# Linear attention, routed experts and a gated layer in one kernel: small loads moved to another queue, norms regrouped, rank products and w1 splits reordered

## The chip, the cores and the metric

One core of a Trainium2 chip runs the whole program. Its engines are PE (TensorE: matrix products and transposes into PSUM), ACT (ScalarE), DVE (VectorE), POOL (GpSimd) and SP (SyncE, which here only issues transfers); transfers run on 16 DMA engines. The metric is the time of one execution on the device in microseconds (us); less is better.

## The reference

```python
# attention without softmax, 4 batches x 8 heads x 576 tokens x 64
kv  = einsum('bhsd,bhse->bhde', k, v)
out = einsum('bhsd,bhde->bhse', q, kv)
x   = out / sqrt(mean(out*out, -1) + 1e-6) * g_norm       # -> 2304 tokens x 512

# 8 experts, the best two of each token
noisy = x @ w_gate + log1p(exp(x @ w_noise)) * noise
top2, top2_w = best two of noisy, softmax over them
x = sum over the two: top2_w * (relu(x @ w1[e]) @ w2[e])  # w1 512x1024, w2 1024x512

# gated layer
h = x @ w_in                                              # 512 x 2048
return (h * sigmoid(h)) @ w_out                           # 2048 x 512
```

## The kernel before

The 2304 tokens are handled as two halves, b = 0 and 1, of 1152 tokens (two attention batches each): 128 partitions times J = 9 tokens. JJ = 5 units `jj` hold tokens 2jj and 2jj+1, the last one only token 8.

**Loads.** `load_qkv(b)` (line 123) issues 8 pairs of k and v and then 8 loads of q on SP's queue, 288 KB each. In program order come then, on the same queue, `gcol` (g_norm, lines 135 and 136), the two halves of `wg_raw` (w_gate and w_noise, lines 138 and 139), `noise_sb` (line 650) and `load_qkv(1)`. Two DVE operations make `gw`, the gate weights times g_norm (line 144).

**Attention.** `kv_of` makes the products of k and v of one batch, `turn_kv` transposes them, `gates_of` multiplies them with `gw`, so that the gate's logits come out of the same product as the attention output; it therefore needs `gw`. `q_of` transposes two tokens' q by PE into `qT`, which ACT copies out of PSUM. `out_of(b, jj, hf)` makes half a unit of the output: 8 heads in two halves of four, so a full half takes 16 short products, ACT's copy `o` (line 435), ACT's square `sq` (line 439) and DVE's sum `ss` (line 440). `out_all(b, between)` runs the ten halves n = 0 to 9, puts a `q_of` behind each of n = 0, 2 and 4, and calls whatever `between` has for n.

**Norms, routing, lists.** `norm(b, group)` computes 1/sqrt of the mean squares for a group of units by a bit trick and three Newton steps of three DVE operations (lines 480 to 482), then the group's logits (`pl`, line 486, and the reduction `lg`, line 491). The groups are units 0 to 2 (six tokens, after n = 5) and units 3, 4 (three tokens, after the last half). `store_x` scales the output to `xh` (line 450) and SP stores it to `x_dram` (line 456). `route(b)` is a generator run piece by piece by `run(b)`: (1) noisy logits and the best two experts, ending in `rowtot`; (2) the rank product `rk` on PE and, on DVE, the ranks, ending in `ohb` (line 604); (3) the list product `ids_ps` on PE, which gives the token lists, `ids_early` for batch 0 and `ids` for both (line 626); (4) the weights of the two experts. `behind(ins)` keeps instructions of the same engine behind `ins`; `marked[b]` is the last one marked by `norm` or `route`, `listed[b]` the write of the list.

**The turn to the experts.** While batch 1 is ranked, PE works for expert 0 on the tokens of batch 0: `early_x` gathers two tiles by `ids_early` (POOL, line 228), transposes them (`xt`) and ACT scales them to `xe` (line 310); `early_h(f)`, f = 0 to 7, are the first layer's products in full float32, evicted by ACT (line 734); `early_y(a)`, a = 0 and 1, the second layer's, eight steps of two passes each. `early_y(1)` has the transposes of the remaining tiles 2, 3 and 4 of expert 0 between its steps 4, 5 and 6; these tiles are gathered from all of `x_dram` by `ids`. Then `mm1` of expert 0 follows, which needs w1 of expert 0 split in a high part (ACT, line 202) and a low part (DVE, line 203).

**Order.** PE runs in the order of the program. ACT and DVE run in that order only where `act` and `dve` are used; where the text has `nc.scalar` or `nc.vector`, a planner that simulates the time line orders them. Behind the turn come eight experts and the gated layer, which the change does not touch.

Of the kernel before, what the change touches and what calls it, by code (L numbers as in the profile page):

```python
# [8 lines left out]
F32 = mybir.dt.float32  # L9
# [5 lines left out]
ALU = mybir.AluOpType  # L15
# [4 lines left out]
P = 128  # L20
PT = 128
# [26 lines left out]
def attention_moe_mlp(  # L48
# [15 lines left out]
    nc = tc.nc  # L64
    pe, act, dve = (InOrder(tc, engine) for engine in (nc.tensor, nc.scalar, nc.vector))

    NB, H, SB, D = q.shape
    B, S = NB // 2, 2 * SB
    N, DM = out.shape
    E, _, F = w1.shape  # L70
    DFF = w_in.shape[1]
    J = S // PT
    JJ = (J + 1) // 2
# [22 lines left out]
    def psB(name):  # L96
        return psum.tile([P, 512], F32, tag="B", name=name)
# [35 lines left out]
    make_identity(nc, ident)  # L133
    gcol = const.tile([P, 1], F32, name="gcol")
    for r in range(2):
        nc.sync.dma_start(gcol[r * D : (r + 1) * D, :], g_norm.rearrange("(d o) -> d o", o=1))
    wg_raw = const.tile([P, HP, 2, E], F32, name="wg_raw")
    nc.sync.dma_start(wg_raw[:, :, 0, :], w_gate.rearrange("(c p) e -> p c e", p=P))
    nc.sync.dma_start(wg_raw[:, :, 1, :], w_noise.rearrange("(c p) e -> p c e", p=P))
    gw = const.tile([P, HP, 4 * E], F32, name="gw")  # L140
    nc.vector.memset(gw, 0.0)
    for r in range(2):
# [75 lines left out]
    def behind(ins):  # L218
        return tc.issue_after(ins.ins) if ins else ExitStack()
# [43 lines left out]
    def store_y(e, a, py, eng):  # L263
        y = mp.tile([P, DM], F32, tag="y", name=f"y{e}_{a}", bufs=2)
        eng.activation(y, py, AF.Copy)
        if a < HA // P:
            eng.dma_start(y_first[e * HA + a * P : e * HA + (a + 1) * P, :], y)
        eng.dma_start(y_dram[e * CAP + a * P : e * CAP + (a + 1) * P, :], y)
# [38 lines left out]
    def early_x():  # L307
        for a in range(HA // P):
            xv = turn_x(gather_x(0, a, x_dram[0 : EB * S, :], ids_early[:, a : a + 1]), psB(f"xt0_{a}"))
            nc.scalar.activation(xe[:, :, a * P : (a + 1) * P], xv, AF.Identity, scale=gcol)  # L310

    raw1, raw2, h0 = [], [], []
    listed, marked, stored = {}, {}, []

    def early_y(a, between):

        py = psB(f"py0_{a}")
        for f in range(KF):
            if f in between:
                between[f]()  # L320
            pe.matmul(
                py, h0[f][:, a * P : (a + 1) * P], raw2[f // 2][:, f % 2 * DM : (f % 2 + 1) * DM],
                start=(f == 0), stop=(f == KF - 1),
            )
        store_y(0, a, py, nc.scalar)

    with ExitStack() as ph1:
        att = ph1.enter_context(tc.tile_pool(name="att", bufs=1))
        wk = ph1.enter_context(tc.tile_pool(name="wk", bufs=2))
# [48 lines left out]
        def q_of(b, jj):  # L378

            j0 = min(2 * jj, J - 2)  # L380
            qps = psA(f"qps{b}_{jj}")
            for r in range(2):
                for hp in range(HP):
                    pe.transpose(
                        qps[:, r, hp * P : (hp + 1) * P],
                        qkv["q", 2 * b + r, hp][:, j0 : j0 + 2, :].rearrange("p j d -> p (j d)"),
                        ident,
                    )
            qT[b, jj] = att.tile([P, 2, HP * P], F32, tag="qT", name=f"qT{b}_{jj}", bufs=3)
            nc.scalar.activation(qT[b, jj], qps, AF.Copy)  # L390
# [21 lines left out]
        def tokens_of(jj):  # L412

            return 2 * jj, min(2, J - 2 * jj)

        def out_of(b, jj, hf):

            j0, n = tokens_of(jj)
            if hf == 0:
                raw[b, jj] = att.tile([P, H, n * 80], F32, tag=f"o{n}", name=f"o{b}_{jj}", bufs=4 if n > 1 else 1)  # L420
            if b not in ss:
                ss[b] = wk.tile([P, J, H], F32, name="ss")
            po = psA(f"po{b}_{jj}_{hf}")
            w = n * 80
            for m in range(4):
                h = hf * 4 + m
                for r in range(2):
                    pe.matmul(
                        po[r * D : (r + 1) * D, m // 2, (m % 2) * w : (m % 2 + 1) * w],
                        qT[b, jj][:, r, h * D : (h + 1) * D],  # L430
                        kvbds[2 * b + r][:, h, 160 - w :],
                        start=True, stop=True,
                    )
            rows = raw[b, jj][:, hf * 4 : (hf + 1) * 4, :]
            nc.scalar.activation(
                rows.rearrange("p (a c) d -> p a (c d)", a=2), po[:, :, : 2 * w], AF.Copy
            )
            sq = wk.tile([P, 4, n, D], F32, tag="sq", name="sq", bufs=2)
            nc.scalar.activation(sq, rows.rearrange("p h (r c) -> p h r c", r=n)[:, :, :, :D], AF.Square)
            nc.vector.tensor_reduce(  # L440
                ss[b][:, j0 : j0 + n, hf * 4 : (hf + 1) * 4].rearrange("p r h -> p h r"),
                sq, axis=AX.X, op=ALU.add,
            )
# [17 lines left out]
        def norm(b, jjs):  # L461

            if b not in rinv:
                rinv[b] = wk.tile([PT, J, H], F32, name="rinv")
                logits[b] = wk.tile([PT, J, 2 * E], F32, name="lg", bufs=1)
            units = [tokens_of(jj) for jj in jjs]
            js = slice(units[0][0], sum(units[-1]))
            nj = js.stop - js.start

            ms = wk.tile([PT, 6 * H], F32, name="ms", bufs=1)[:, : nj * H]  # L470
            nc.vector.tensor_scalar(
                ms, ss[b][:, js].rearrange("p j h -> p (j h)"), 1.0 / D, EPS, op0=ALU.mult, op1=ALU.add
            )
            rf = rinv[b][:, js].rearrange("p j h -> p (j h)")
            ri = rf.bitcast(I32)
            nc.vector.tensor_single_scalar(ri, ms.bitcast(I32), 1, op=ALU.arith_shift_right)
            nc.vector.tensor_scalar(ri, ri, -1.0, float(0x5F3759DF), op0=ALU.mult, op1=ALU.add)
            t0 = wk.tile([PT, 6 * H], F32, name="t0", bufs=1)[:, : nj * H]
            for _ in range(3):
                nc.vector.tensor_mul(t0, rf, rf)  # L480
                nc.vector.scalar_tensor_tensor(t0, t0, -0.5, ms, op0=ALU.mult, op1=ALU.mult)
                nc.vector.scalar_tensor_tensor(rf, t0, 1.5, rf, op0=ALU.add, op1=ALU.mult)

            pl = wk.tile([P, 6, H, 2 * E], F32, name="pl", bufs=1)[:, :nj]
            for jj, (j0, n) in zip(jjs, units):
                nc.vector.tensor_mul(
                    pl[:, j0 - js.start : j0 - js.start + n],
                    raw[b, jj].rearrange("p h (r c) -> p r h c", r=n)[:, :, :, D:],
                    rinv[b][:, j0 : j0 + n, :, None].to_broadcast([P, n, H, 2 * E]),
                )  # L490
            marked[b] = nc.vector.tensor_reduce(logits[b][:, js], pl.rearrange("p j h c -> p j c h"), axis=AX.X, op=ALU.add)

        def route(b):
# [153 lines left out]
            yield  # L647

        noise_sb = const.tile([PT, B, J, E], F32, name="noise_sb")
        nc.sync.dma_start(  # L650
            noise_sb.rearrange("p b j e -> p b (j e)"),
            noise.rearrange("(b p j) e -> p b (j e)", b=B, j=J),
        )
# [3 lines left out]
        def run(b):  # L657
            if b not in step:
                step[b] = route(b)
            next(step[b])  # L660

        GROUPS = (range(3), range(3, JJ))

        def out_all(b, between):

            for n in range(2 * JJ):
                out_of(b, *divmod(n, 2))
                if n % 2 == 0 and n // 2 + 2 < JJ:
                    q_of(b, n // 2 + 2)
                if n in between:  # L670
                    between[n]()
                if n == 5:
                    norm(b, GROUPS[0])

        def store_behind(b, jjs):
            with behind(marked[b]):
                store_x(b, jjs)
# [9 lines left out]
        gates_of(1)  # L687
        q_of(0, 1)
        out_all(0, {})
        norm(0, GROUPS[1])  # L690
        store_behind(0, (0,))
        run(0)
# [13 lines left out]

        def rank_first():
            run(0)
            store_behind(0, GROUPS[1])

        out_all(1, {2: rank_first, 5: lambda: run(0)})
        early_x()
        norm(1, GROUPS[1])
        store_behind(1, (0,))
        run(1)
# [19 lines left out]

        for f in range(KF):
            early_h(f)
            if f == 6:
                run(1)
                store_behind(1, GROUPS[1])  # L740
        early_y(0, {3: lambda: run(1)})
        with behind(marked[B - 1]):
            w1_sb[0] += [split(raw1[c], f"w1_0_{c}", nc.scalar, nc.vector) for c in range(KD)]
        with behind(listed[B - 1]):
            run(B - 1)
# [555 lines left out]
```

## Time and profile before

| | before |
|---|---|
| median of 3 runs | 1001.96 us (1001.76 to 1007.46) |
| the profiled execution, whole | 995.8 us |
| its span, first to last instruction | 994.0 us |
| PE busy | 955.5 us (96%) |
| DVE busy | 500.3 us (50%) |
| ACT busy | 327.9 us (33%) |
| POOL busy | 252.1 us (25%) |
| mean granted clock of PE | 0.992 |

A busy share is a mean over the whole span; a stage can look different. In a time line, a row has the start and the length in us, the engine (SPq is SP's queue), the line of the source (L44 is the helper through which all ordered instructions are recorded), the operation, what it writes and reads, and how many rows of the same kind were merged; in brackets how long the engine had been idle and what ended that. Float32 products run as two passes and count twice. PEclk is the granted clock as a share of 2.4 GHz: 1.00 is 2.4 GHz, 0.50 is 1.2 GHz.

### The profile page before, as it was taken

Reading aid. Unit: us, or ns where it says so; the run is one execution under the profiler, and the core shown is the slowest. Engines: PE = TensorE matmul, PEld = TensorE weight load, DVE = VectorE, ACT = ScalarE, POOL = GpSimd, SP = SyncE. Lnnn points to the kernel's source line nnn. Section 1 sums busy time; section 2 is a strip of 40 time slices with the busy share of each in tenths; the row PEclk is TensorE's granted clock in tenths of the full one; section 3 lists DMA queues with packets and bytes.
Section 4 is the critical chain, followed back from the end, with each engine's and each line's share of the span. In section 5 each row is a group of like instructions: output and inputs, shape, how many; then the busy total and the mean of one; then the engine's idle time right before and its main releaser. Section 6 shows DMA issues by size and latency. Waiting matters only on the chain. (4 is left out here: it accounts for less than half of the span.)

```text
span 994.0 us, 14472 instructions
## 1 busy us (share of the span) xinstructions
PE 955.5 (96%) x5586; PEld 818.1 (82%) x5586; DVE 500.3 (50%) x949; ACT 327.9 (33%) x499; POOL 252.1 (25%) x271
## 2 busy tenths in 40 slices
PE   5988899999999999999999999999999999999997
PEld 4867599889798897989889789888888888888886
DVE  2488648675766766666674355332333332232221
ACT  1773254333333333333333244222321231223212
POOL 3000255535444454544520131001100010100000
PEclk9998999999999999999999999999999999999999
DMA  9862637484755747466471573101110020101001
GB/s 318 282 233 76 215 121 232 141 273 126 235 180 161 242 128 253 150 202 199 131 246 49 165 226 94 43 1 43 40 46 21 22 85 1 43 1 43 0 1 44
DMA packets 65096, 127.01 MB, mean 128 GB/s; under 512 B 11264, under 2 KB 19456, under 8 KB 65024
## 3 DMA queue, kind: packets, MB, share of 16 engines
q1 hardware_dynamic: 50880, 91.44, 28.6%
q0 software_dynamic: 6080, 19.93, 6.5%
q10 hardware_dynamic: 8064, 14.68, 4.0%
q8 instruction: 45, 0.74, 0.3%
q14 instruction: 27, 0.22, 0.1%
HBM read 92.94 MB, written 33.08 MB: 127 GB/s over the span
## 5 line engine op out<-in xcount | busy, mean ns | idle before, releaser
L44 PE MATMUL ph<-xT,hw 128*128 128x256 f32 (+1 forms) x960 | 212.5, 312 | 0.1
L44 PE MATMUL py<-hw,h 128*128 128x512 f32 x608 | 199.8, 400 | 7.6 <-DVE h L44 5.4
L44 PE MATMUL pout<-hwout,g 128*128 128x512 f32 x576 | 191.8, 395 | 0.0
L44 PE MATMUL pg<-x2T,hwin 128*128 128x512 f32 (+1 forms) x640 | 184.2, 373 | 0.0
L44 PEld LDWEIGHTS ph<-xT,hw 128*128 128x128 f32 x960 | 162.6, 189 | 1.8 <-DVE xT L44 0.6
L44 DVE TENSOR_TENSOR sg<-pg,sg 128x512 f32<-128x512 f32 x72 | 49.8, 692 | 211.0 <-ACT sg L44 211.0
L44 PE MATMUL ph<-xT,lw 128*128 128x256 f32 (+1 forms) x480 | 149.8, 312 | 0.0
L44 PEld LDWEIGHTS py<-hw,h 128*128 128x128 f32 x608 | 114.4, 188 | 35.5 <-DVE h L44 8.1
L44 PEld LDWEIGHTS pg<-x2T,hwin 128*128 128x128 f32 x640 | 116.6, 189 | 23.4 <-DVE x2T L44 0.2
L44 PEld LDWEIGHTS pout<-hwout,g 128*128 128x128 f32 x576 | 108.2, 188 | 24.3
L44 PE MATMUL py<-lw,h 128*128 128x512 f32 x304 | 119.9, 394 | 0.0
L44 PE MATMUL pg<-x2T,lwin 128*128 128x512 f32 (+1 forms) x320 | 119.0, 372 | 0.0
L44 ACT ACTIVATE sg<-pg 128x512 f32<-128x512 f32 x72 | 43.1, 598 | 217.1 <-PE pg L44 217.1
L44 PE MATMUL pout<-lwout,g 128*128 128x512 f32 x288 | 112.9, 392 | 0.0
L1010 POOL DMA_INDIRECT yg<-y_dram,rt x32 | 31.8, 993 | 261.1 <-PE x2ps L44 219.0
L44 DVE SCALAR_TENSOR_TENSOR h<-ph,h 128x640 fp32r<-128x640 f32 (+1 forms) x64 | 50.5, 789 | 82.5 <-ACT h L44 78.2
L44 ACT ACTIVATE h<-ph 128x640 fp32r<-128x640 f32 (+1 forms) x64 | 43.5, 679 | 144.3 <-PE ph L44 135.7
L44 PEld LDWEIGHTS ph<-xT,lw 128*128 128x128 f32 x480 | 90.6, 189 | 0.0
L1093 POOL TENSOR_TENSOR w<-w,bits 128x256 f32<-128x256 f32 x64 | 47.3, 740 | 143.4 <-DVE w L44 143.2
L44 DVE TENSOR_TENSOR g<-sg,g 128x512 fp32r<-128x512 f32 x72 | 49.8, 692 | 44.7 <-ACT g L44 44.7
L203 POOL TENSOR_TENSOR lw<-rw,hw 128x1024 fp32r<-128x1024 f32 x28 | 67.4, 2409 | 17.0 <-ACT hw L44 17.0
L44 PEld LDWEIGHTS pg<-x2T,lwin 128*128 128x128 f32 x320 | 60.4, 189 | 11.5
(173 smaller groups left out, 1082.4 us busy)
## 6 DMA issues: line engine op xcount, KB each, us to landing
rw<-in_moe_w_dram SPq DMA_DIRECT2D x56, 512.0 KB, 4.0
y_dram<-y ACTq DMA_DIRECT2D x40, 256.0 KB, 4.1
f<-in_moe_w_in_dram SPq DMA_DIRECT2D x32, 256.0 KB, 3.6
f<-in_moe_w_out_dram SPq DMA_DIRECT2D x32, 256.0 KB, 3.0
k<-in_k_dram SPq DMA_DIRECT2D x16, 288.0 KB, 6.0
v<-in_v_dram SPq DMA_DIRECT2D x16, 288.0 KB, 6.3
q<-in_q_dram SPq DMA_DIRECT2D x16, 288.0 KB, 6.0
out_dram<-ob SPq DMA_DIRECT2D x18, 256.0 KB, 3.5
```

The source lines that it names most:

```text
L44: return lambda *args, **kwargs: self.tc.keep_in_program_order(op(*args, **kwargs))
L203: low.tensor_sub(lo, raw, hi.bitcast(F32))
L1010: nc.gpsimd.indirect_dma_start(out=y, out_offset=None, in_=src, in_offset=bass.IndirectOffsetOnAxis(ap=self.rt[:, t, kk : kk + 1].bitcast( ...
L1093: nc.gpsimd.tensor_add(w, w, bits.bitcast(F32))
```

## The change

Five small loads (`gcol` twice, `wg_raw` twice, `noise_sb`) are issued from ScalarE's queue instead of SP's. A norm's group 0 now has units 0 and 1 (four tokens, computed after half n = 3), group 1 units 2 to 4 (five tokens). The three Newton steps (nine operations) become a third-order step and one Newton step (seven operations); the buffers shrink from six to five tokens. In batch 1's `out_all` the rank product of batch 0 moves from behind half 2 to behind half 0, and the list product from behind half 5 to behind half 3. The rank product of batch 1 moves from behind `early_h(6)` to behind `early_h(7)`, its list product from before step 3 to before step 6 of `early_y(0)`. The stores behind them keep their units 3 and 4. The splits of w1 of expert 0 stand behind `listed` instead of `marked`, so on DVE behind the write of the lists instead of behind `ohb`.

```diff
--- before.py
+++ after.py
@@ -133,10 +133,10 @@
     make_identity(nc, ident)
     gcol = const.tile([P, 1], F32, name="gcol")
     for r in range(2):
-        nc.sync.dma_start(gcol[r * D : (r + 1) * D, :], g_norm.rearrange("(d o) -> d o", o=1))
+        nc.scalar.dma_start(gcol[r * D : (r + 1) * D, :], g_norm.rearrange("(d o) -> d o", o=1))
     wg_raw = const.tile([P, HP, 2, E], F32, name="wg_raw")
-    nc.sync.dma_start(wg_raw[:, :, 0, :], w_gate.rearrange("(c p) e -> p c e", p=P))
-    nc.sync.dma_start(wg_raw[:, :, 1, :], w_noise.rearrange("(c p) e -> p c e", p=P))
+    nc.scalar.dma_start(wg_raw[:, :, 0, :], w_gate.rearrange("(c p) e -> p c e", p=P))
+    nc.scalar.dma_start(wg_raw[:, :, 1, :], w_noise.rearrange("(c p) e -> p c e", p=P))
     gw = const.tile([P, HP, 4 * E], F32, name="gw")
     nc.vector.memset(gw, 0.0)
     for r in range(2):
@@ -467,7 +467,8 @@
             js = slice(units[0][0], sum(units[-1]))
             nj = js.stop - js.start
 
-            ms = wk.tile([PT, 6 * H], F32, name="ms", bufs=1)[:, : nj * H]
+
+            ms = wk.tile([PT, 5 * H], F32, name="ms", bufs=1)[:, : nj * H]
             nc.vector.tensor_scalar(
                 ms, ss[b][:, js].rearrange("p j h -> p (j h)"), 1.0 / D, EPS, op0=ALU.mult, op1=ALU.add
             )
@@ -475,13 +476,16 @@
             ri = rf.bitcast(I32)
             nc.vector.tensor_single_scalar(ri, ms.bitcast(I32), 1, op=ALU.arith_shift_right)
             nc.vector.tensor_scalar(ri, ri, -1.0, float(0x5F3759DF), op0=ALU.mult, op1=ALU.add)
-            t0 = wk.tile([PT, 6 * H], F32, name="t0", bufs=1)[:, : nj * H]
-            for _ in range(3):
-                nc.vector.tensor_mul(t0, rf, rf)
-                nc.vector.scalar_tensor_tensor(t0, t0, -0.5, ms, op0=ALU.mult, op1=ALU.mult)
-                nc.vector.scalar_tensor_tensor(rf, t0, 1.5, rf, op0=ALU.add, op1=ALU.mult)
-
-            pl = wk.tile([P, 6, H, 2 * E], F32, name="pl", bufs=1)[:, :nj]
+            t0 = wk.tile([PT, 5 * H], F32, name="t0", bufs=1)[:, : nj * H]
+            nc.vector.tensor_mul(t0, rf, rf)
+            nc.vector.tensor_mul(t0, t0, ms)
+            nc.vector.scalar_tensor_tensor(t0, t0, -10.0 / 3.0, t0, op0=ALU.add, op1=ALU.mult)
+            nc.vector.scalar_tensor_tensor(rf, t0, 5.0, rf, op0=ALU.add, op1=ALU.mult)
+            nc.vector.tensor_mul(t0, rf, rf)
+            nc.vector.scalar_tensor_tensor(t0, t0, -27.0 / 1024.0, ms, op0=ALU.mult, op1=ALU.mult)
+            nc.vector.scalar_tensor_tensor(rf, t0, 9.0 / 16.0, rf, op0=ALU.add, op1=ALU.mult)
+
+            pl = wk.tile([P, 5, H, 2 * E], F32, name="pl", bufs=1)[:, :nj]
             for jj, (j0, n) in zip(jjs, units):
                 nc.vector.tensor_mul(
                     pl[:, j0 - js.start : j0 - js.start + n],
@@ -647,7 +651,7 @@
             yield
 
         noise_sb = const.tile([PT, B, J, E], F32, name="noise_sb")
-        nc.sync.dma_start(
+        nc.scalar.dma_start(
             noise_sb.rearrange("p b j e -> p b (j e)"),
             noise.rearrange("(b p j) e -> p b (j e)", b=B, j=J),
         )
@@ -659,7 +663,7 @@
                 step[b] = route(b)
             next(step[b])
 
-        GROUPS = (range(3), range(3, JJ))
+        GROUPS = (range(2), range(2, JJ))
 
         def out_all(b, between):
 
@@ -669,7 +673,7 @@
                     q_of(b, n // 2 + 2)
                 if n in between:
                     between[n]()
-                if n == 5:
+                if n == 3:
                     norm(b, GROUPS[0])
 
         def store_behind(b, jjs):
@@ -706,9 +710,9 @@
 
         def rank_first():
             run(0)
-            store_behind(0, GROUPS[1])
-
-        out_all(1, {2: rank_first, 5: lambda: run(0)})
+            store_behind(0, (3, 4))
+
+        out_all(1, {0: rank_first, 3: lambda: run(0)})
         early_x()
         norm(1, GROUPS[1])
         store_behind(1, (0,))
@@ -735,11 +739,11 @@
 
         for f in range(KF):
             early_h(f)
-            if f == 6:
+            if f == 7:
                 run(1)
-                store_behind(1, GROUPS[1])
-        early_y(0, {3: lambda: run(1)})
-        with behind(marked[B - 1]):
+                store_behind(1, (3, 4))
+        early_y(0, {6: lambda: run(1)})
+        with behind(listed[B - 1]):
             w1_sb[0] += [split(raw1[c], f"w1_0_{c}", nc.scalar, nc.vector) for c in range(KD)]
         with behind(listed[B - 1]):
             run(B - 1)
```

## Rows read from the trace of the kernel before

**Rows 1.** Timeline of PE, first 63 us: start, length, instruction, [idle before, releaser]

```profile
16.76 1.26 PE L44 MATMUL kv<-v,k 64*64 64x64 f32 x36 [0.24 <-DMA v<-in_v_dram]
...
24.27 1.03 PE L44 MATMUL gp_ps<-gw,kvT 128*64 128x32 f32 x8 [6.24 <-DVE gw L144]
...
25.85 1.97 PE L44 MATMUL qps<-ident,q 128*128 128x128 f32 x8
...
30.20 1.31 PE L44 MATMUL po<-kvbd,qT 128*64 128x160 f32 x16
...
59.56 1.09 PE L44 MATMUL qps<-ident,q 128*128 128x128 f32 x8
...
62.54 1.31 PE L44 MATMUL po<-kvbd,qT 128*64 128x160 f32 x16
```

**Rows 2.** Timeline of SP's queue, the same columns

```profile
10.44 6.54 SPq L123 DMA_DIRECT2D q<-in_q_dram  x8
```

**Rows 3.** Timeline of ACT: its first eviction

```profile
11.27 0.78 ACT L372 ACTIVATE kvs<-kv 64x256 f32<-64x256 f32 x2 [9.27 <-PE kv L44]
```

**Rows 4.** DMA issues, 16.3 to 17.2 us: KB each, median us to landing

```profile
q<-in_q_dram SPq DMA_DIRECT2D x1, 288.0 KB, 6.0
```

**Rows 5.** DMA queues, 20.4 to 22.6 us: packets, MB, share

```profile
q1 hardware_dynamic: 1375, 0.23, 73.1%
```

**Rows 6.** Windows: busy us by engine, PEclk, DMA share, GB/s

```profile
24.00:26.00 2.00, 1.74 (x13) 1.58 (x14) 1.25 (x4) 0.32 (x2) 0.00 (x0) 0.50 0.86 241
...
88.00:90.00 2.00, 2.00 (x6) 1.55 (x6) 1.66 (x10) 0.00 (x0) 0.00 (x0) 0.50 0.00 0
```

**Rows 7.** Timeline of PE, 84 to 119 us

```profile
84.09 0.66 PE L44 MATMUL xt<-ident,xg 128*128 128x128 f32 x4 [1.33 <-DMA xg<-x_dram,ids_early]
...
87.19 14.04 PE L44 MATMUL ph<-xe,r 128*128 128x256 f32 x56 [0.78 <-ACT xe L310]
...
106.83 2.87 PE L44 MATMUL ids_ps<-eat,ohb 128*128 128x80 bf16 x18 [0.89 <-DVE ohb L604]
...
109.52 7.91 PE L44 MATMUL py<-r,h 128*128 128x512 f32 x18
...
118.44 0.63 PE L44 MATMUL xt<-ident,xg 128*128 128x128 f32 x4 [1.01 <-DMA xg<-x_dram,ids]
```

**Rows 8.** Timeline of ACT: two evictions of early_h, with three more between them

```profile
92.64 0.38 ACT L734 ACTIVATE h<-ph 128x256 f32<-128x256 f32 x1 [0.74 <-PE ph L44]
...
99.54 0.38 ACT L734 ACTIVATE h<-ph 128x256 f32<-128x256 f32 x1 [0.40 <-PE ph L44]
```

**Rows 9.** Timeline of DVE, 62 to 114 us

```profile
62.26 0.29 DVE L533 TENSOR_REDUCE rowtot<-wide 128x8 bf16<-128x72 bf16 x1
...
84.04 0.42 DVE L440 TENSOR_REDUCE ss<-sq 128x4 f32<-128x256 f32 x1
...
99.96 0.29 DVE L533 TENSOR_REDUCE rowtot<-wide 128x8 bf16<-128x72 bf16 x1
...
105.42 1.35 DVE L604 TENSOR_TENSOR ohb<-iota_b,low_b 128x2304 bf16<-128x2304 bf16 x1
...
106.69 1.82 DVE L450 TENSOR_TENSOR xh<-o,rinv 128x1024 f32<-128x1024 f32 x2
...
108.42 3.49 DVE L203 TENSOR_TENSOR lw<-r,hw 128x1024 fp32r<-128x1024 f32 x3
...
113.11 0.19 DVE L626 SCALAR_TENSOR_TENSOR ids<-ids_sum 128x40 int32<-128x40 f32 x1
```

**Rows 10.** Groups of DVE instructions, 43 to 54 us: busy, mean ns, idle

```profile
L491 DVE TENSOR_REDUCE lg<-pl 128x96 f32<-128x768 f32 (+1 forms) x2 | 2.3, 1131 | 0.0
...
L482 DVE SCALAR_TENSOR_TENSOR rinv<-t,rinv 128x48 f32<-128x48 f32 (+1 forms) x6 | 1.2, 194 | 0.2
```

**Rows 11.** Timeline of POOL: the first gather of expert 0's later tiles

```profile
114.04 1.01 POOL L228 DMA_INDIRECT xg<-x_dram,ids  x1 [10.24 <-DVE dm L634]
```

**Rows 12.** DMA issues, 107.5 to 109 us: KB each, median us to landing

```profile
x_dram<-xh SPq DMA_DIRECT2D x1, 512.0 KB, 2.7
```

## The prediction

> **What bounds the kernel now.** I read the windows first, then what PE waits for, then PE's timeline of the first 126 us, and only then the other engines at the places where PE stood still. PE is what the span is made of: after the first 126 us it hardly waits, and no edit touches that part, so I carry it over unchanged. The places to win are the holes of the head. The largest is in the first stage: the last product of `kv_of` starts at 16.76 us and takes 1.26, then PE stands 6.24 us for `gw` (line 144), and runs its next products at half rate: the 8 transposes of `q_of(0, 0)` take 1.97 us where the same 8 take 1.09 later [rows 1], and the granted clock around them is 0.50, the 1.2 GHz level [rows 6]. `gw` needs `gcol` and `wg_raw`, and SP issues those behind 24 loads of q, k and v; the last eight alone hold SP's queue from 10.44 to 16.98 us [rows 2].
>
> The second group of holes is at the turn from attention to expert 0's first products. PE ends `out_all(1)` at 84.09 - 1.33 = 82.76 us, waits for the gather of `early_x`, and starts `early_h` only at 87.19; the first part of `early_h` again runs at the 0.50 clock [rows 6, 7]. The third is the list of batch 1: the product that makes it waits 0.89 us for `ohb`, and the gathered tiles that follow come 1.01 us late [rows 7]. From 84 to 113 us DVE works without a break on the norms and ranks of batch 1, and writes `ids` only at 113.30, though the list product ended by 109.52: the splits of w1 (line 203) stand in between [rows 7, 9].
>
> **The change, part by part.** *Small loads on ScalarE's queue.* ACT evicts nothing before 11.27 us; it sat idle 9.27 us before that [rows 3]. SP's eight q loads took 6.54 / 8 = 0.82 us of issue each [rows 2]; five issues at that price are 4.1 us, inside ACT's idle time. If that cover were gone, ACT's first eviction would move by what sticks out, and it is not on the path until the last q has landed. The small loads are then there long before `gates_of(0)` wants them. What is late next is q: the last q load is issued by about 16.7 us and lands 6.0 us later, at 22.7 [rows 2, 4]. It is pushed back by the small packets, which now go ahead of it. Those are the bulk of the 1375 packets of 20.4 to 22.6 us, which used 73.1% of the 16 DMA engines, 0.731 x 2.2 = 1.6 us [rows 5]. So the push is between 0 and 1.6 us; the two streams partly fill each other's gaps, and I take 0.6. Then q is whole at 23.3, the transposes end some 0.3 later at 23.6 instead of 25.85 + 1.97 = 27.82. From the end of `q_of` to the first product of `out_of` batch 1 needs 62.54 - (59.56 + 1.09) = 1.9 us at the full clock; batch 0 needed 30.20 - 27.82 = 2.4 [rows 1]. First `out_of` product at 25.5 instead of 30.20: **-4.7 us**. Bounds: no push, 22.7 + 0.3 + 1.9 = 24.9, -5.3; full push and the half clock kept, 22.7 + 1.6 + 0.3 + 2.4 = 27.0, -3.2; loads no earlier at all, 0. SP's queue, freed of five issues, starts the loads of batch 1 sooner; nobody waits for those.
>
> Here a rule speaks against the edit. The Trainium skill (DMA: Bandwidth & Descriptors, "Issuing engines are not separate DMA queues") says that transfers started by any engine share the same 16 DMA engines, and that a second issuing engine saves only issue time. By that alone the first term would be 0; the sum by the rows is the one above.
>
> *Ranks of batch 0, two `out_of` halves earlier.* The rank product and the list product of batch 0 move forward together past two halves of `out_of` and one `q_of`, 2 x 1.31 + 1.09 = 3.7 us of PE [rows 1], and keep the same PE work between them, so the wait for `ohb` there stays. What hangs on them (the last `xh`, its store, the gather of `early_x`) comes 3.7 us earlier against PE, more than the 1.33 us that PE waited [rows 7]. Left of the 82.76 to 87.19 stretch (4.4 us) are two times four transposes at 0.66 [rows 7], then ACT's last `xe`, which stands behind the evictions of `out_of`; I allow 1.2 us for it, from the 0.78 that PE waited there [rows 7] and some queueing. 4.4 - 2.5: **-1.9 us** (bounds: -2.3 with 0.78, and 0 if the gather keeps its distance).
>
> *Clock.* The 56 products of `early_h` took 14.04 us [rows 7]. Four later steps of eight took 99.54 - 92.64 = 6.9 us [rows 8], 1.725 each, so 56 at the full clock are 12.1. The clock fell after a stretch of waits that is now largely gone: **-1.9 us** (or 0).
>
> *Norms.* Two of nine steps go from each norm at 0.19 us each [rows 10], 0.4 us of DVE. The first norm of a batch covers four tokens and starts after half 3, where DVE still has idle time. The second grows to five tokens. In batch 1 the last sum of squares ends at 84.46, 1.7 us after PE's last `out_of`, and `rowtot` at 100.25, 15.8 us later [rows 9]; in that time DVE also finishes the first group, whose reduction alone is about 1.1 us [rows 10], with its products and most steps. I take 13.6, between 15.8 and 12.7.
>
> Now the pieces meet. With -4.7, and 0.2 given back where ACT starves around the moved list product, PE ends `out_all(1)` at 78.2; `early_h` starts at 80.8 and ends 8 x 1.725 = 13.8 later, at 94.6. `rowtot` is at 78.2 + 1.7 + 13.6 = 93.5. So the rank product of batch 1, put behind the eighth step instead of the seventh, finds its input ready (at 15.8 it would wait 1.1). `ohb` follows `rowtot` by 106.77 - 100.25 = 6.5 us [rows 9]: 100.0. PE reaches the list product after the rank product (some 0.3) and six steps of `early_y`, 12 passes at 7.91 / 18 = 0.44 [rows 7]: 100.2. The wait of 0.89 goes: **-0.8 us**.
>
> *w1 splits behind the list.* Three subtractions of 3.49 us together [rows 9] and a fourth no longer stand before `ids`. They then run behind it, 4 x 1.16 = 4.7 us, from 103.6 to 108.3, while DVE would be idle; the next DVE work on the path is the split of the first gathered tile at about 111. If the list came 3 us later they would delay that split one for one. The list product ends at 100.2 + 2.7 = 102.9. The gather needs `ids` and the last rows of x: two `xh`, 1.82 us together, behind `ohb` [rows 9], then a store that lands in 2.7 us [rows 12], with handovers 105.4. From the gather's start to the first transpose took 118.44 - 114.04 = 4.4 us [rows 7, 11]: 109.8. PE has less left to fill with, 20 passes instead of 26, 12 of them before that tile: it wants it at 102.9 + 5.3 = 108.2 and waits 1.6 instead of 1.01: **+0.6 us**. Had the splits stayed in front, the gather would start near 107 and this term be +2.2.
>
> **Sum.** -4.7 - 1.9 - 1.9 - 0.8 + 0.6 = -8.7 us. The profiled execution ran 995.8 us with a span of 994.0: 985.3 of span. The timed runs have their median 6 us higher, at 1001.96; the same difference there gives **993.3 us**.
>
> **Rivals.** *More* (0.24): the small packets displace nothing, `xe` follows at once, and DVE is early enough that the later gather costs no wait: -5.3, -2.3, and -1.0 in place of +0.6: -11.3, 990.7. For it: the 16 engines are not full in 20.4 to 22.6 [rows 5]. Against: the store of x bounds the later gather, whatever the lists do.
>
> *The small loads come no sooner* (0.12): ACT's issues queue behind SP's backlog, 6.54 us for eight [rows 2], and their packets behind the bulk. Then -4.7 goes: -4.0, 998.0. For it: the DMA engines are shared. Against: ACT is free from 11.27 - 9.27 = 2.0 us [rows 3], before that backlog builds up. This is the case the Trainium skill's rule (same page and section) would give.
>
> *The moved rank product waits* (0.04): it now stands in PE's queue before everything that follows half 0, some 2.4 us after 62.54, while `rowtot` of batch 0 ended at 62.55 [rows 1, 9]. If DVE's chain did not move with PE, it would be 4.7 - 2.4 = 2.3 us late: -6.4, and if batch 1's chain slid too, near 997.
>
> *Slower* (0.04): the clock stays at 1.2 GHz through the whole of `early_h`. Its 64 products would take 2 x 13.8 us: -8.7 + 13.8 = +5.1, 1007.1. It decides if PE's pauses before 80.8 lower the clock as those before 87.19 did; it then came back after a few us [rows 6, 8], which speaks against.
>
> *The forecast* has the remaining 0.56.
>
> **Numbers.** A measurement of this kernel tells about 1% from no change, so 991.9 and 1012.0 are the edges. Faster by over 1%: the first rival and the upper edge of the forecast, 0.30. Slower: the clock rival with further lost terms, 0.05. Within: 0.65. The forecast's own range is 991.5 to 996; with the first two rivals and a little spread of the measurement, 989 to 1000 leaves out no more than 2 in 10.
>
> **What would show it.** PE's wait for `gw` is gone, the first `po` stands near 25.5, and q is the last releaser before it; the granted clock is 1.00 there. `early_h` starts near 80.8 with a wait on ACT's `xe`, not on the gather. `ids` directly follows the list product near 103.5, with line 203 behind it, and the first late tile's transpose is near 110, released by the gather. I am wrong if `gw` still ends PE's wait after 22 us, if the rank products wait for `rowtot`, or if the head shrinks and the part behind 126 us grows.

## The result and the profile after

The changed kernel ran in 993.11 us (median of 9 runs, 989.71 to 995.82), the kernel before beside it in 1001.96: ratio 0.991, 95% interval 0.9886 to 0.9934. The forecast was 993.3. The profiled execution of the changed kernel took 992.24 us with a span of 990.4, which is its kernel's usual time. The profiled one of before took 995.8, 6 us less than its median. So the pair of traces shows only -3.6 us of the timed -8.9, and the difference between the two figures is a finding of its own (below). Three executions are left out of all figures because they took far longer than any other of their kernels: 1345.86 and 1062.31 us of the kernel before, 2412.67 us of the variant with `noise_sb` on SP.

PE's timeline after the change, first part (start, length, instruction, idle before and its releaser), beside [rows 1]:

```profile
19.52 0.65 PE L44 MATMUL gp_ps<-gw,kvT 128*64 128x32 f32 x8
21.27 0.46 PE L44 MATMUL kvT_ps<-ident,kvs 64*128 64x64 f32 x4 [1.11 <-DVE kvbd L375]
...
24.92 0.33 PE L44 MATMUL qps<-ident,q 128*128 128x128 f32 x1 [0.43 <-DMA q<-in_q_dram]
25.18 0.94 PE L44 MATMUL gp_ps<-gw,kvT 128*64 128x32 f32 x8
26.05 1.97 PE L44 MATMUL qps<-ident,q 128*128 128x128 f32 x8
27.95 1.69 PE L44 MATMUL po<-kvbd,qT 128*64 128x160 f32 x16
...
43.45 6.77 PE L44 MATMUL kv<-v,k 64*64 64x64 f32 x214
52.32 0.27 PE L44 MATMUL kv<-v,k 64*64 64x64 f32 x2 [2.09 <-issue]
52.52 0.59 PE L44 MATMUL kvT_ps<-ident,kvs 64*128 64x64 f32 x4
53.04 3.67 PE L44 MATMUL kv<-v,k 64*64 64x64 f32 x72
...
61.71 1.31 PE L44 MATMUL po<-kvbd,qT 128*64 128x160 f32 x16
```

The wait of 6.24 us for `gw` is gone: `gp_ps` starts at 19.52. PE now waits for q, piece by piece, to 24.92. Then the transposes take 1.97 us for eight, the half rate of [rows 1] again. The first `po` comes at 27.95 instead of 30.20. At 52.32 stands a pause of 2.09 us without a releaser; before had one of 2.64 at the same place. Behind it the 72 products of `kv` take 3.67 us instead of 2.31.

SP's and ACT's queues after, first 13 us (start, length of the issue):

```profile
2.11 0.59 SPq L123 DMA_DIRECT2D v<-in_v_dram  x1
3.79 0.33 SPq L123 DMA_DIRECT2D k<-in_k_dram  x1
4.97 0.33 SPq L123 DMA_DIRECT2D v<-in_v_dram  x1
6.31 0.33 SPq L123 DMA_DIRECT2D k<-in_k_dram  x1
6.84 0.33 SPq L123 DMA_DIRECT2D v<-in_v_dram  x1
8.15 0.33 SPq L123 DMA_DIRECT2D k<-in_k_dram  x1
...
12.16 6.37 SPq L123 DMA_DIRECT2D q<-in_q_dram  x8
...
0.76 1.19 ACTq L136 DMA_DIRECT2D gcol<-in_g_norm_dram  x2
1.99 0.61 ACTq L138 DMA_DIRECT2D wg_raw<-in_moe_w_gate_dram  x1
...
4.04 0.38 ACTq L654 DMA_DIRECT2D noise_sb<-in_moe_noise_dram  x1
```

ACT's five issues are over by 4.42 us and cost ACT nothing. But four of SP's issues now begin 1.2 to 1.7 us behind the one before (of the sixteen issues of k and v in before, no two in a row began more than 0.8 apart), and the q loads start at 12.16, 1.72 us later than in [rows 2].

Windows of the changed kernel (busy us by engine, PEclk, DMA share, GB/s), beside [rows 6]:

```profile
24.00:26.00 2.00, 1.41 (x10) 1.08 (x10) 0.00 (x0) 0.71 (x1) 0.00 (x0) 0.84 1.06 394
26.00:28.00 2.00, 2.00 (x12) 1.62 (x10) 0.28 (x1) 0.47 (x2) 0.00 (x0) 0.50 1.05 391
...
54.00:56.00 2.00, 2.00 (x44) 2.00 (x42) 1.78 (x7) 0.00 (x0) 0.00 (x0) 0.50 1.03 347
...
88.00:90.00 2.00, 2.00 (x11) 1.74 (x11) 1.97 (x4) 1.04 (x4) 0.00 (x0) 1.00 0.00 0
...
544.00:546.00 2.00, 1.90 (x5) 1.51 (x6) 0.23 (x1) 0.00 (x0) 0.00 (x0) 0.55 0.84 240
```

The window of 88 to 90 us, at 0.50 in before, is at 1.00. New stretches at 1.2 GHz stand at 54 and, in code that the change doesn't touch, at 544 us.

PE's timeline at the turn, beside [rows 7]; then DVE and POOL, beside [rows 9, 11]:

```profile
81.75 1.09 PE L44 MATMUL xt<-ident,xg 128*128 128x128 f32 x8
84.27 14.08 PE L44 MATMUL ph<-xe,r 128*128 128x256 f32 x64 [1.43 <-ACT xe L310]
98.19 0.20 PE L44 MATMUL rk<-rowtot,ones 128*128 128x72 bf16 x1
...
104.04 2.87 PE L44 MATMUL ids_ps<-eat,ohb 128*128 128x80 bf16 x18
106.73 7.03 PE L44 MATMUL py<-r,h 128*128 128x512 f32 x12
113.59 0.63 PE L44 MATMUL xt<-ident,xg 128*128 128x128 f32 x4
```

```profile
83.67 0.42 DVE L440 TENSOR_REDUCE ss<-sq 128x4 f32<-128x256 f32 x1 [0.22 <-ACT sq L439]
...
97.18 0.28 DVE L537 TENSOR_REDUCE rowtot<-wide 128x8 bf16<-128x72 bf16 x1
...
107.22 0.20 DVE L630 SCALAR_TENSOR_TENSOR ids<-ids_sum 128x40 int32<-128x40 f32 x1
107.34 1.22 DVE L203 TENSOR_TENSOR lw<-r,hw 128x1024 fp32r<-128x1024 f32 x1
...
109.64 1.01 POOL L228 DMA_INDIRECT xg<-x_dram,ids  x1 [8.62 <-DMA x_dram<-xh]
```

Nothing waits for the early gather any more, neither list nor rank product of batch 1 waits, and `ids` follows its product at once, with line 203 behind it. `mm1` of expert 0 starts at 118.94 instead of 124.35: 5.4 us won in the head. Of these, 1.8 are lost again behind it: the stretch at 1.2 GHz from 544 us costs 1.7 (windows 544 to 548 stand at 0.55 and 0.60, 2 x (0.45 + 0.40)), PE then waits 1.83 us for `yg` where it waited 0.98, and some 0.7 come back by the end.

### The profile page after: what moved, and what is told of

Its sections match the earlier page's. It is cut to its first block, busy times and chain, and to the rows that moved or that the text cites. A ratio compares the mean times of both kernels' runs of the same rounds, so it can differ in the third digit from the quotient of the medians.

```text
span 990.4 us, 14460 instructions
## 1 busy us (share of the span) xinstructions
PE 958.6 (97%) x5586; PEld 819.8 (83%) x5586; DVE 499.0 (50%) x941; ACT 327.5 (33%) x499; POOL 253.1 (26%) x271
```

## The experiments

All are given as the ratio to the kernel before, timed beside them on the same chip. Each execution also has its span and mean granted clock; (1 - clock) x span is a measure of the time lost to the lower clock (an upper one, since a low clock while PE stands still costs nothing; the clock is known to 0.001, about 1 us of a single run), and the rest of the span is what the order of the work costs at 2.4 GHz. Means over the runs. The first four variants ran on one chip, the two repeats of the changed kernel on two others, and the mean spans of before differ by up to 1.7 us between the groups; a difference of mean spans across groups is no surer than that:

| kernel | ratio, 95% interval | span | lost to clock | rest |
|---|---|---|---|---|
| before (four groups, 11 to 35 runs each) | 1 | 998.2 to 999.9 | 13.5 to 15.5 | 983.7 to 985.2 |
| changed | 0.991 (0.9886 to 0.9934) | 991.6 | 10.4 | 981.3 |
| changed_again | 0.9924 (0.9897 to 0.995) | 991.2 | 9.9 | 981.3 |
| changed_third | 0.9935 (0.9911 to 0.9959) | 991.4 | 10.6 | 980.8 |
| loads_only | 0.9976 (0.9954 to 0.9997) | 995.8 | 12.5 | 983.4 |
| without_loads | 0.9978 (0.9956 to 1.0) | 995.7 | 13.9 | 981.8 |
| without_pe_order | 0.9977 (0.9958 to 0.9997) | 995.6 | 12.0 | 983.5 |
| splits_before_list | 0.9969 (0.9947 to 0.9991) | 995.9 | 12.5 | 983.3 |
| old_norms | 0.9945 (0.9924 to 0.9966) | 994.6 | 10.9 | 983.7 |
| q_before_gates | 0.9927 (0.9904 to 0.995) | 991.8 | 10.6 | 981.2 |
| late_weight_loads | 0.9915 (0.9885 to 0.9945) | 990.6 | 9.7 | 980.9 |
| weights_behind_x | 0.9895 (0.9872 to 0.9919) | 988.0 | 9.1 | 978.9 |
| weights_behind_x_noise_sp | 0.9911 (0.9885 to 0.9936) | 989.4 | 9.7 | 979.7 |
| weights_behind_x_again | 0.9905 (0.9876 to 0.9934) | 989.2 | 8.1 | 981.1 |

Before's profiled execution lost only 994.0 x (1 - 0.992) = 8.0 us to the clock: that is the 6 us by which it lay under its median.

**The queue alone.** The kernel before with the five loads on ScalarE's queue.

```diff
-    nc.sync.dma_start(gcol ...); nc.sync.dma_start(wg_raw ...); nc.sync.dma_start(noise_sb ...)
+    nc.scalar.dma_start(gcol ...); nc.scalar.dma_start(wg_raw ...); nc.scalar.dma_start(noise_sb ...)
```

> The kernel before with one edit: the five small loads go to ScalarE's queue. Theory A (the terms of the prediction): PE's first product of out_of comes 4.7 us earlier and nothing later takes it back, so about 997.3 us, a ratio of 0.995. Theory B (what the two profiles suggest: that product came only 2.3 us earlier, and the first product of batch 1 only 0.8 us): the small packets push the large loads back and most of the gain is gone before batch 1, so 1000 to 1001.5, a ratio of 0.998 to 1.000. In the profile A wants q landed by 23.3 us, B by about 25.

The first `po` came at 28.13 us, with q's last wait ending at 24.83, as theory B had it; the ratio is 0.9976, 2.4 us, between the two theories. The head gives the gain back at old waits. PE reached the early gather, the list product and the later tiles earlier, and waited there:

```profile
85.72 0.66 PE L44 MATMUL xt<-ident,xg 128*128 128x128 f32 x4 [1.04 <-DMA xg<-x_dram,ids_early]
...
108.78 2.87 PE L44 MATMUL ids_ps<-eat,ohb 128*128 128x80 bf16 x18 [1.33 <-DVE ohb L604]
120.33 0.63 PE L44 MATMUL xt<-ident,xg 128*128 128x128 f32 x4 [0.96 <-DMA xg<-x_dram,ids]
123.59 0.63 PE L44 MATMUL xt<-ident,xg 128*128 128x128 f32 x4 [1.78 <-DMA xg<-x_dram,ids]
```

**All but the queue.** The changed kernel with the five loads back on SP.

```diff
-    nc.scalar.dma_start(gcol ...)   # and wg_raw, noise_sb
+    nc.sync.dma_start(gcol ...)
```

> The changed kernel with the five small loads back on SP's queue. Theory A: 993.1 + 4.7 = about 998, ratio 0.996. Theory B: 994 to 995, ratio 0.992 to 0.993, with PE's wait for gw of 6.2 us back in the profile and the turn to expert 0 still without a wait for the gather of early_x.

The old wait is back, and two thirds to three quarters of the whole change's gain are gone (0.9978, more than either theory allowed; the whole change gave 0.991 to 0.9935):

```profile
25.00 1.03 PE L44 MATMUL gp_ps<-gw,kvT 128*64 128x32 f32 x8 [6.68 <-DVE gw L144]
```

Against the whole change the rest of the span grew by 0.5 us and the time at the lower clock by 3.5. In this profile every window of 2 us from 20 to 36 us lies under the full clock, 0.50 in most, so PE also works slowly behind the wait of 6.7 us: from the first `po` to the next product of k and v it needs 48.16 - 31.37 = 16.8 us, where the changed kernel needs 15.5.

**All but PE's order.** The rank and list products at their old places.

```diff
-        out_all(1, {0: rank_first, 3: lambda: run(0)})
+        out_all(1, {2: rank_first, 5: lambda: run(0)})
-            if f == 7:
+            if f == 6:
-        early_y(0, {6: lambda: run(1)})
+        early_y(0, {3: lambda: run(1)})
```

> The changed kernel with the rank and list products of both batches back at their old places in PE's order (behind halves 2 and 5, behind early_h(6), before step 3 of early_y(0)). Theory A: the wait for the gather of early_x, the half clock in early_h and the wait for ohb come back, 1.9 + 1.9 + 0.8 us, less 1.1 for the longer fill behind the list product: about 996.5, ratio 0.995. Theory B: the order carries nearly all of the gain, 999 to 1000, ratio 0.997 to 0.998.

PE waits for the early gather again, and a later tile comes late:

```profile
85.34 0.66 PE L44 MATMUL xt<-ident,xg 128*128 128x128 f32 x4 [1.08 <-DMA xg<-x_dram,ids_early]
86.90 0.66 PE L44 MATMUL xt<-ident,xg 128*128 128x128 f32 x4 [0.90 <-DMA xg<-x_dram,ids_early]
...
122.83 1.07 PE L44 MATMUL xt<-ident,xg 128*128 128x128 f32 x4 [2.03 <-DMA xg<-x_dram,ids]
```

The ratio, 0.9977, is that of theory B. The mean span is 4.0 us longer than that of the whole change, 2.3 in the rest and 1.7 at the clock.

**All but the splits.** Line 203 before the list again.

```diff
-        with behind(listed[B - 1]):
+        with behind(marked[B - 1]):
             w1_sb[0] += [split(raw1[c], f"w1_0_{c}", nc.scalar, nc.vector) for c in range(KD)]
```

> The changed kernel with the splits of w1 of expert 0 again only behind ohb, not behind the write of the lists. Theory A: ids is written about 2 us later, but the gather then waits for ids instead of the store of x, and PE has fill: 1.6 us of loss, 994.7, ratio 0.9925. Theory B (the list edit carries much of it): 996 or more, ratio 0.994 or more.

Ratio 0.9969, as theory B had it. Two tiles now come late:

```profile
119.35 0.63 PE L44 MATMUL xt<-ident,xg 128*128 128x128 f32 x4 [1.65 <-DMA xg<-x_dram,ids]
...
124.17 0.94 PE L44 MATMUL xt<-ident,xg 128*128 128x128 f32 x4 [2.04 <-DMA xg<-x_dram,ids]
```

The rest of the span is 2.1 us longer than with the whole change, the time lost to the clock 2.2.

**The changed kernel again.** No edit.

> The changed kernel itself, beside the next three on one chip. Both theories: ratio 0.991 as in its first runs (0.9886 to 0.9934). The four partial kernels each kept only 0.2 to 0.3% of a gain of 0.9%. Theory A (independent terms that add up) would want the parts to sum to the whole; theory C (the granted clock: pauses of PE in the head lower it, and most of the spread between executions and part of the gain is clock) wants the mean granted clock of this kernel above that of the kernel before, 0.989 or more against 0.986, and span less clock loss only 2 to 4 us shorter.

Ratio 0.9924, with the same split of its span (981.3 and 9.9). Its mean granted clock was 0.990 beside 0.985 of before, and its span less the clock loss was 3.0 us shorter, as theory C had it.

**All but the norms.** Old groups, three Newton steps, the moved rank products kept.

```diff
-        GROUPS = (range(2), range(2, JJ))
+        GROUPS = (range(3), range(3, JJ))
-                if n == 3:
+                if n == 5:
# and the three Newton steps and the buffers of six tokens, as before
```

> The changed kernel with the old norms: groups of six and three tokens, the first after half 5, three Newton steps. Theory A: the last sum of squares to rowtot of batch 1 takes 15.8 us again instead of 13.5; PE reaches the rank product at about the same time, so it waits 1 us for rowtot and 0.8 us more for ohb: 995 us, ratio 0.993. Theory B (the norms matter for the first gather too, since DVE is busier between the list of batch 0 and the last half): ratio 0.995 or more.

Ratio 0.9945, 3.0 us above the changed kernel timed beside it (996.43 against 993.44) and between the two theories. DVE ends later than PE now asks:

```profile
99.25 0.43 PE L44 MATMUL rk<-wide,same 128*128 128x72 bf16 x8 [0.58 <-DVE wide L531]
106.10 2.87 PE L44 MATMUL ids_ps<-eat,ohb 128*128 128x80 bf16 x18 [1.04 <-DVE ohb L604]
```

**The other way to the same end.** The loads stay on SP, but PE does the transposes of q before the gates' products, so it doesn't stand before `gw`; batch 0's list product moves one half further back.

```diff
-        gates_of(0)
         turn_kv(1)
         q_of(0, 0)
-        gates_of(1)
         q_of(0, 1)
+        gates_of(0)
+        gates_of(1)
-        out_all(1, {0: rank_first, 3: lambda: run(0)})
+        out_all(1, {0: rank_first, 4: lambda: run(0)})
```

> The changed kernel with the small loads back on SP's queue, but the two first transposes of q ahead of the two products with gw in PE's order, and the list product of batch 0 behind half 4 instead of 3. If the large loads are what the first stage is bound by, the small loads behind them cost nothing once PE has the transposes to do: first product of out_of near 26.3 us instead of 27.9, and the wait of 0.83 us for ohb of batch 0 gone: 2 us better than the changed kernel, ratio 0.989. If the early small loads are what helps, it falls back to the ratio of the kernel without them, 0.998.

Ratio 0.9927, against 0.9924 of the changed kernel beside it: no difference. The run has two edits, so it doesn't tell what PE's order alone is worth. With the loads back on SP, q was whole 2.1 us sooner than in the changed kernel (its last wait ends at 22.79, there at 24.92), and the first `po` came at 26.74:

```profile
22.79 2.18 PE L44 MATMUL qps<-ident,q 128*128 128x128 f32 x9 [0.21 <-DMA q<-in_q_dram]
```

The list product of batch 0 no longer waited 0.83 us for `ohb`, but the early gather did come late again, 0.69 and 0.81 us.

**The pause without a releaser.** The eight loads of w1 and w2 of expert 0 (512 KB each), which run while `kv_of(3)` pauses, are held back: w1 behind the first, w2 behind the third store of x of batch 0.

```diff
+        with behind(stored[0]):
             raw1 += [fetch(w1_rows(0, c), "", None, wslot(f"r1_{c}", F32)) for c in range(KD)]
+        with behind(stored[-1]):
             raw2 += [fetch(w2_rows(0, i), "", 2, wslot(f"r2_{i}", F32)) for i in range(KF // 2)]
```

> The changed kernel with the eight loads of w1 and w2 of expert 0 (4 MB) held back on SP's queue: w1's behind the store of the first unit of x of batch 0, w2's behind the third. Theory D: PE's pause of 2.1 to 2.6 us at the end of the first part of kv_of(3), where nothing that it waits for is shown, is its own instruction fetch standing behind those 4 MB on the DMA engines; then the pause goes, the clock does not fall at 52 us, and the time is 2 to 3.5 us below the changed kernel. Rival: the pause has nothing to do with the weight loads and stays; same time within 1 us.

The pause is gone: the 216 products run through, and 1.1 us of wait for ACT is what is left.

```profile
42.56 6.51 PE L44 MATMUL kv<-v,k 64*64 64x64 f32 x216
50.21 0.46 PE L44 MATMUL kvT_ps<-ident,kvs 64*128 64x64 f32 x4 [1.13 <-ACT kvbd L345]
...
79.72 1.12 PE L44 MATMUL xt<-ident,xg 128*128 128x128 f32 x4 [1.64 <-DMA xg<-x_dram,ids_early]
```

The time, 0.9915 against 0.9924, shows no gain: the early gather was issued at 76.19 us, 1.0 later than in the changed kernel though PE was 3.8 us ahead at the rank product of batch 0, and PE waited 1.64 us for it; the clock fell there as well (four transposes in 1.12 us).

**Both behind the first store.**

```diff
+        with behind(stored[0]):
             raw1 += ...
+        with behind(stored[0]):
             raw2 += ...
```

> The changed kernel with all eight loads of w1 and w2 of expert 0 behind the store of the first unit of x of batch 0. In the run with w2's loads behind the third unit the pause of 2.1 to 2.9 us at the end of the first part of kv_of(3) was gone and PE was 3.4 us ahead at the rank product of batch 0, but the stores of x and so the gather of early_x then stood behind w2's 2 MB, and PE waited 1.9 us for it with a lower clock in early_h. Theory D: here the 4 MB are through before the last stores of x of batch 0, so the gather is on time and the 3 us stay: 2.5 to 3.5 us below the changed kernel, ratio 0.989. Rival: the pause comes back since the loads again start while PE fetches, or the gather is late again: the changed kernel's ratio, 0.991 to 0.992.

Ratio 0.9895, 989.79 us. The pause is gone here too, and the first store of x lands sooner. Issues between 40 and 56 us, of the changed kernel and then of this one (KB each, median us to landing):

```profile
x_dram<-xh SPq DMA_DIRECT2D x1, 512.0 KB, 10.9
```

```profile
x_dram<-xh SPq DMA_DIRECT2D x1, 512.0 KB, 3.6
```

```profile
43.91 6.94 PE L44 MATMUL kv<-v,k 64*64 64x64 f32 x216
51.55 0.46 PE L44 MATMUL kvT_ps<-ident,kvs 64*128 64x64 f32 x4 [0.70 <-ACT kvbd L345]
```

**The same, with `noise_sb` on SP.**

```diff
-        nc.scalar.dma_start(  # noise_sb
+        nc.sync.dma_start(
```

> As the run beside it, but with the noise load back on SP's queue behind q, so that 72 KB less stand before the last load of q. If each small packet ahead of q costs PE its time, the last q lands 0.2 to 0.4 us earlier and the time is that much lower; if the small packets are hidden, no difference: within 0.5 us of the run beside it.

Ratio 0.9911: nothing that can be told from 0.9895. PE's last wait for q ended at 24.62 us, not sooner than the 24.40 of the run beside it, so it isn't `noise_sb` that pushes q.

**The better version and the changed kernel on one chip.**

> The changed kernel once more, beside the version with the weight loads behind the first x store, on one chip. Theory (the pause at the end of the third product of k and v, 2.1 to 2.9 us, comes with the eight weight loads of 512 KB, and holding these back also lets the first x store land sooner): 0.991 to 0.993 of the kernel before, span less low-clock time about 981. Rival (the earlier lead of 3.5 us was the chip or the low clock of that call): within 1 us of the version beside it.

> The changed kernel with the loads of w1 and w2 of expert 0 issued behind the first x store. Theory: 2 to 3.5 us less than the changed kernel beside it, span less low-clock time about 979, no pause without a releaser at the last two products of the first part of the third k and v product. Rival: within 1 us of the changed kernel.

Medians 992.36 and 991.13, ratios 0.9935 and 0.9905, with intervals that overlap. Again no pause with the loads held back, 2.36 us of it without. But the lead is 1.2 us of median and 2.2 of mean span (991.4 and 989.2), at the low end of what was expected or below it, and here it lies in the time lost to the clock (8.1 against 10.6), not in the rest. In its trace PE, with the pause gone, waits 2.68 us for the first late tile. Both runs of the version with the held loads have a lower ratio (0.9895, 0.9905) than all three of the changed kernel (0.991 to 0.9935); that it is faster by 1 to 3 us is likely and not settled.

## Why the prediction was right, and where it was not

**Small loads: right in kind, too large.** `gw` no longer holds PE. But the first `po` came 2.25 us earlier, not 4.7. Two steps failed. The step "the push is between 0 and 1.6 us" counted the packets of the small loads; PE's last wait for q ended at 24.92, about 2.2 us later than the 22.7 of no push; with the loads on SP (`q_before_gates`) it ended at 22.79. Most of that push was there before q's loads were issued: SP's issues of k and v stood further apart between 2.1 and 8.2 us, and q's issue began 1.72 us later. The prediction had carried q's issue over unchanged. The gaps stand in the traces with the loads on ScalarE's queue (`after`, `changed_again`, `loads_only`, `weights_behind_x`) and not in before, `without_loads` or `q_before_gates`; what holds SP up in them no run shows. And the step that took the rest at the full clock was wrong: behind PE's waits of 1.11 us for `kvbd` and then 0.26 to 0.50 us each for q, the clock still fell (0.84, then 0.50).

The rule weighed in the prediction (the Trainium skill, DMA: Bandwidth & Descriptors, "Issuing engines are not separate DMA queues") gave 0 for this term. The trace doesn't bear that out: without the moved loads the change was worth 0.0022 instead of 0.009. Yet the kernel with the loads on SP, another PE order and a later list product reached the same time. So the queue mattered here by the place that it gave the loads in the order of issue, and because PE had nothing else to do meanwhile.

**The early gather: right.** POOL issued it at 75.17, PE didn't wait, and ACT's `xe` cost 1.43 us where 1.2 was allowed. `early_h` started 84.27 - 81.75 = 2.5 us behind `out_all(1)`, as the sum had it (4.4 - 1.9).

**Clock in `early_h`: right.** 64 products in 14.08 us at 1.00, predicted 13.8. The run without the new order went back to 14.04 for 56, the time of [rows 7], and the two variants in which PE waited for the early gather again (`q_before_gates`, `late_weight_loads`) took 15.77 and 15.66 for 64.

**Norms, rank, list of batch 1: right.** From the last sum of squares to `rowtot` 97.46 - 84.09 = 13.4 us, predicted 13.6, before 15.8. No wait for `rowtot`, none for `ohb`. The run with old norms waits 0.58 (for `wide`, just ahead of `rowtot`) and 1.04; 1.1 and 0.9 were named. One reading was off: the 1.1 us taken for the first group's reduction is a mean over both groups' shapes [rows 10]; in the turn of before that reduction took 1.44 us.

**The splits and the later gather: right in place, a little low in price.** The store of x bounds the gather (109.64), as said. The wait before the first tile was 0 in the profiled execution because PE ran at 1.2 GHz from about 107 to 111 us (12 passes of `py` in 7.03 us); in the second trace of the changed kernel, at the full clock (5.33 us for the 12), it was 2.55, predicted 1.6:

```profile
114.76 0.63 PE L44 MATMUL xt<-ident,xg 128*128 128x128 f32 x4 [2.55 <-DMA xg<-x_dram,ids]
```

Undoing the edit cost 4.2 us of mean span where the prediction had 1.6.

**The sum and its carrying over: two errors that met.** Against before's own profiled execution, 985.3 us of span were predicted and 990.4 measured. Of these 5.1 us, 2.5 are the first term (2.25 for 4.7). Another 1.4 went at `kv_of(3)`: the pause there stood in the trace of before, I carried it over without a term, and the 72 products behind it, at 1.2 GHz this time, took 3.67 us for 2.31. (The pause itself was 0.55 shorter than in before.) In the untouched part 1.8 were lost where I had nothing; that this part would grow was one of the signs of being wrong that the prediction named. And some 0.6 came back at the second late tile, whose wait fell from 1.35 to 0.78. The step that failed in the other direction is the last one, which added the 6 us between the profiled execution and the median as if they were fixed. They were time at the lower clock (8.0 us lost in the profiled execution, about 14 in the others on the mean), and the change removed part of it: 10.4 us are left. So of the 7 to 9 us between the means, about 3 are in the rest of the span and 4 to 6 in the clock. The median of 993.11 beside a forecast of 993.3 is the meeting of two errors of opposite sign, each of about 5 us: that it is so close is luck.

**The rivals.** *More* didn't come about: the push was larger, not nil. *No sooner* fell: `gp_ps` started at 19.52. *The rank product waits* fell: `rk` of batch 0 ran at 63.88 without a wait. *Slower* fell: the clock of `early_h` was 1.00.

**The parts don't add up.** Undoing one of four parts costs 3.0 to 4.2 us of mean span, 15 together, where the whole is worth 7 to 9. Each part removes a wait that the others would only move PE into: an earlier PE that still waits for the gather, or for `ohb`, gains neither the wait nor the clock behind it.

## What to carry to other kernels

Where several short waits follow one another, take them together: the moved loads alone gave 2.4 us of mean span, while undoing them in the whole cost 4.1, since PE otherwise stands at the next wait. Before carrying a sum from one profiled execution to a median, compare that execution's granted clock with those of the timed ones. And where a small load is late, look first for work that the engine can do meanwhile; here a kernel with such an order, and one more edit, was as fast as the one with another queue.

## What the runs showed of the hardware that was not expected

**A pause with no releaser that went with the bulk loads.** In each trace with the eight weight loads at their old place, PE stood still before the last one or two products of the first part of `kv_of(3)`, 2.1 to 2.9 us (before 2.64, changed 2.09, again 2.88 and 2.36). In the four with the loads held back, all 216 products ran through. That the loads bring it is shown. The DMA view has an instruction queue, q8, with now and then one packet of 0.02 MB; the one near the pause stands in the same words in before (52 to 54 us) and in the changed kernel (48 to 50 us):

```profile
q8 instruction: 1, 0.02, 3.0%
```

Read in windows of 0.05 us, it stands at 52.25 us in before, and PE goes on at 54.58; in the changed kernel at 49.90, and PE goes on at 52.32. In all ten traces with the pause PE goes on 2.2 to 2.5 us behind this packet, wherever between 49.9 and 55.7 us it stands. Five of them (`changed_third`, `loads_only`, `without_loads`, `splits_before_list`, `old_norms`) have a shorter pause without a releaser, 0.30 to 0.53 us, some 6 us earlier, and there PE goes on 2.4 to 2.5 us behind the q8 packet before that. With the eight loads at their old place the two packets are 6.1 to 6.9 us apart, with the loads held back 3.5 to 3.8, and there the 216 products end 2.8 to 3.0 us behind the second, without a stop. So the pause is most likely PE waiting for its own instructions, which come late behind the bulk; that q8 serves PE is inferred from this nearly fixed distance, since no run changed that queue alone. The Trainium skill (Runtime: NRT & Kernel Launch, "Instruction fetch mechanics") says that instructions are refilled in blocks of 16 KiB by a DMA queue of the sequencer and that this is mostly hidden; if the pause is that refill, it was not hidden here.

**Much of the spread from run to run is the clock.** The mean granted clock of before lay between 0.978 and 0.992, which is 8 to 22 us of the span. In three of the four groups the span varied by 2.1 to 2.7 us and the rest of it, without the time lost to the clock, by 1.3 to 1.4 (standard deviations); in the largest group, of 35 runs, the rest varied by 2.4 and the span by 2.2, so there the clock doesn't account for it. In the changed kernel a stretch at 1.2 GHz began at about 25 us, behind waits of 1.11 us and then of 0.26 to 0.50 each. Such a stretch comes in one execution and not in the next at the same wait: PE's wait of 2.14 us for `rt`, which ends at 549.5 us in before and at 544.1 in the changed kernel, stands in both traces, and only in the changed kernel were the products behind it slow.
